# One run of small products a period: results of one pair of chunks together with the scores of the next, and sums that change PSUM halves

## The chip, the cores and the metric

The kernel runs on one core of a Trainium2 chip. The metric is device time in microseconds (us); the figure shown for a kernel is the median of its runs. Engines are named as in the profile: PE (TensorE, the matrix products), DVE (VectorE), ACT (ScalarE), POOL (GpSimd) and SP (SyncE, which here only issues DMAs).

## What is computed

A recurrent retention block feeds a feed-forward block. Four batches, eight heads, 768 positions, head size 64; 3072 tokens, model width 512, inner width 2048.

```python
for t in range(S):
    state = gamma[None, :, None, None] * state + np.einsum('bhd,bhe->bhde', k[:, :, t], v[:, :, t])
    y[:, :, t] = scale * np.einsum('bhd,bhde->bhe', q[:, :, t], state)
...
x = np.ascontiguousarray(attn_out.transpose(0, 2, 1, 3)).reshape(B * S, H * D)
...
h = x @ w_in
sp = np.maximum(h, 0.0) + np.log1p(np.exp(-np.abs(h)))
g = h * erf(sp)
return (g @ w_out).astype(np.float32)
```

## The kernel before, in words

**Chunks and groups.** The positions are cut into 24 chunks of 128 (six a batch). Two chunks make a group of 256 tokens, so there are 12 groups. A chunk j of the retention is done in two steps with small f32 products of 64x64 on PE.

- `begin(j)` (L560 to L576) makes the scores (L566, kT by qT) and the new contributions to the state (L573, k by v) for both halves of 64 positions. They fill two banks of PSUM.
- `states(j)` (L578 to L593), on DVE, masks the scores into `am` (L582) and adds the contributions to the running state (L591, L593).
- `results(j)` (L595 to L631) multiplies q with the state (L611) and the masked scores with v (L622) into two banks, and ACT copies the result to `xT` (L630). The second half's share of the first half's keys lies in a part of the bank of its own; `crossed_sums` (L633) adds it on DVE (L639, L641).
- `split_x` (L643) splits `xT` into three parts, x_hi on ACT (L314), x_lo and x_dif on DVE (L315, L316), in a ring of three groups.

**Units and periods.** From group 2 on, the hidden layer is computed in units. A unit (`pair_unit`, L712) multiplies two groups of tokens, 512 columns, with 128 columns of w_in in 12 products of 128x512 (L720): eight into one bank (the hi and lo parts) and four into a second (the dif part). Its `put` (L728) reads both banks, the first on ACT (L322), the second on DVE (L323), into a buffer `h` in SBUF, and POOL issues its store (L731). Period g is eight units (`period`, L936; periods 2 and 12 have four units of `unit`, L687, each with 24 products of 256 columns, L693). The periods' loop stands from L1000 on. What goes with each unit is written by hand in `period`: one table of PE work ahead of a unit, one of work for the other engines behind it. Every engine executes its own queue in that order.

In the periods 3 to 9 the table `joined` puts `begin` of both chunks ahead of unit 2, and their `results` ahead of unit 5, so PE leaves the large products twice in a period. In period 10 the two chunks go one by one, four runs of small products. The chunks up to 9 are done alike in both kernels.

**PSUM.** There are eight banks. The units' sums use the four of `ps_o` (o0 to o3), two at a time in turn (`banks`, L680); the retention's scores and results use two banks called hp and two called r.

**Preparation.** `load_pair` (L145) loads k and v of two chunks as they are through POOL's queue (L143, L153), and k and q once more in blocks of 32 through SP's queue (L159, 32 small DMAs a pair), in the units 0 to 2 of the period before their use. `prepare` (L531) transposes the blocks on DVE (L543), scales q (L538), and scales v on ACT (L550, sixteen small instructions a pair). Between all this, DVE and ACT turn w_out from 64-bit into 32-bit numbers in steps (`convert`; DVE lines L230, L244, L249, L253, L265, one step each, five a piece of weights); POOL loads its raw quarters (L208) and stores the pieces (L271).

**Buffers.** `h`, the masks `am` and the output rows share six small buffers of SBUF; most other tiles share 34 larger ones.

**The end.** After the units come the products with w_out (L905), 48 blocks of 24 products, fed by softplus and erf on ACT (L846, L850), a product on DVE (L860) and the same three-way split.

Of the kernel before, what the change touches and what calls it, by code (L numbers as in the profile page):

```python
# [21 lines left out]
P = 128  # L22
C = 128
# [26 lines left out]
def kernel(  # L50
# [39 lines left out]
    def b4(name, shape, dtype=F32):  # L90
        return big.tile([P] + shape, dtype, name=name, tag="b4")
# [22 lines left out]
    def of_chunk(x, j):  # L114

        b, c = divmod(j, NC)
        return x[b, :, c * C : (c + 1) * C, :].rearrange("h p d -> p h d")
# [24 lines left out]
        V[j] = VP[j - j % 2][:, j % 2]  # L142
        queue.dma_start(V[j], of_chunk(v, j))  # L143

    def load_pair(j):  # L145

        b, c = divmod(j, NC)
        KNP[j] = b4("kn", [2, H, D])
        KB[j], QB[j] = (b4(name, [HP, 2 * C]) for name in ("kb", "qb"))
        for i in range(2):  # L150
            load_values(j + i, nc.gpsimd)
            KN[j + i], SLOT[j + i] = KNP[j][:, i], head
            nc.gpsimd.dma_start(KN[j + i], of_chunk(k, j + i))  # L153
        yield
        for to, src in ((KB[j], k), (QB[j], q)):
            for s, d in itertools.product(range(2), range(2)):
                part = slice((2 * s + d) * 32, (2 * s + d + 1) * 32)
                for u in range(HP):
                    nc.sync.dma_start(  # L159
                        to[part, u].rearrange("p (a d) -> p a d", d=32),  # L160
                        src[b, head(u, s), c * C : (c + 2) * C, d * 32 : (d + 1) * 32].rearrange(
                            "(a p) d -> p a d", p=32
                        ),
                    )
                yield

    kq_s = const.tile([P, NC, 2, H], F32, name="kq_s")
    d_k = const.tile([P, H], F32, name="d_k")
# [362 lines left out]
    def prepare(j):  # L531


        for name, store, x in (("k", KT, KB[j]), ("q", QT, QB[j])):
            if name == "q":
                own = x.rearrange("p u (a d) -> p u a d", d=32)
                scale = kq_b[:, 1, :, j % NC : j % NC + 2].rearrange("p u c a -> p u (c a)")
                nc.vector.tensor_tensor(  # L538
                    own, own, scale[:, :, :, None].to_broadcast([P, HP, 8, 32]), op=ALU.mult
                )  # L540
                yield
            t = b4(name + "T", [HP, 2 * C])
# [3 lines left out]
            yield  # L546
        for i in range(2):
# [9 lines left out]
    def additions(j):  # L557
        return range(2 if j % NC < NC - 1 else 1)

    def begin(j, pool=ps_h, names=None):  # L560

        SC[j] = [ret_psum(pool) if names is None else ps_o.tile([P, HP, C], F32, name=names[r]) for r in range(2)]
        for hp in range(HP):
            for a, s in itertools.product(range(2), range(2)):
                t, own = slice(a * D, (a + 1) * D), slice(s * D, (s + 1) * D)
                nc.tensor.matmul(  # L566
                    SC[j][s][t, hp, :D], KT[j][own, hp, t], QT[j][own, hp, t], start=True, stop=True,
                )
        for u in range(HP):
            for r in range(2):  # L570
                for a in additions(j):
                    t = slice(a * D, (a + 1) * D)
                    nc.tensor.matmul(  # L573
                        SC[j][a][r * D : (r + 1) * D, u, D:], KN[j][t, SLOT[j](u, r), :], V[j][t, head(u, r), :],
                        start=True, stop=True,
                    )  # L576

    def states(j):  # L578

        AM[j] = b2("am", [2, HP, D])  # L580
        for s in range(2):
            nc.vector.tensor_tensor(  # L582
                AM[j][:, s],
                SC[j][s][:, :, :D],
                causal_d[:, None, :].to_broadcast([P, HP, D]),
                op=ALU.mult,
            )
        for a in additions(j):
# [6 lines left out]
    def results(j, names=None, pool=ps_r):  # L595

        x = x_of(j)
        pp = [ret_psum(pool) if names is None else ps_o.tile([P, HP, C], F32, name=names[r]) for r in range(2)]
        clear = set()

        def first(*bank):
# [72 lines left out]
        for g in range(2):  # L674
            nc.gpsimd.dma_start(HID[g][:, ft], h[:, g])

    turn = itertools.cycle(range(2))
    last_turn = itertools.cycle((ps_r, ps_h, ps_o, ps_o))
# [113 lines left out]
    def steps(s, n=1):  # L792
# [1 line left out]
            next(s, None)  # L794

    pair = load_pair(JPC + 2)
    prep = prepare(JPC + 2)
    a, b = JPC, JPC + 1
    during = {
        1: [(load_block_scales,)],  # L800
# [10 lines left out]
        12: [(split_weights, 2), (steps, prep, 1)],  # L811
        13: [(steps, prep, 1)],
# [123 lines left out]
    def period(g, prep, next_prep):  # L936

        a, b = 2 * g + 2, 2 * g + 3
        one, two = partial(partial, unit), partial(partial, pair_unit)
        if g == G2:  # L940
            units = [one(g, n) for n in range(NPC // 2)]
            return units, {0: [(results, a), (results, b, None, ps_h)]}, {
                0: [(crossed_sums, a), (crossed_sums, b)],
                1: [(split_x, a, 2)],
                2: [(split_weights, 4)],
                3: [(steps, next_prep, 4)],
            }, range(4)
        if g < NG:
            units = [two(g - 1, ft) for ft in range(8 * (g % 2), 8 * (g % 2) + 8)]
        if g == G2 + 1:  # L950
            return units, joined(2, 5, g), {
                0: [(steps, prep)],
                1: [(split_weights, 5)],
                2: [(states, a), (states, b)],
                3: [(split_weights, 6)],
                4: [(split_weights, 7)],
                5: [(crossed_sums, a), (crossed_sums, b)],
                6: [(split_x, a, 2)],
                7: [(steps, next_prep, 1)],
            }, range(4)  # L960
        if g < NG - 2:
            return units, joined(2, 5, g), {
                0: [(steps, prep, 4)],
                1: [(convert, 2)],
                2: [(states, a), (convert, 1)],
                3: [(states, b), (convert, 1)],
                4: [(convert, 2 if g < 8 else 1)],
                5: [(crossed_sums, a), (crossed_sums, b)],
                6: [(split_x, a, 2)],
                7: [(steps, next_prep, 1 if g < NG - 3 else 4), (convert, 1)],  # L970
            }, LOADS.get(g, ())
        if g == NG - 2:
            return units, {1: [(begin, a)], 2: [(results, a)], 3: [(begin, b)], 5: [(results, b)]}, {
                0: [(steps, prep, 4), (load_w_out, 0)],
                1: [(states, a), (load_w_out, 1)],
                2: [(crossed_sums, a), (split_w_out, 0)],
                3: [(states, b), (split_x, a)],
                4: [(split_w_out, 1), (load_hiddens, 0)],
                5: [(crossed_sums, b)],
                6: [(split_x, b), (softplus, 0), (load_w_out, 2)],  # L980
                7: [(erf, 0), (gated, 0)],
            }, ()
        if g == NG - 1:
# [14 lines left out]
        }, ()  # L998

    for g in range(G2, NG + 1):  # L1000
        pair = load_pair(2 * g + 4) if 2 * g + 4 < NJ else iter(())
        next_prep = prepare(2 * g + 4) if 2 * g + 4 < NJ else iter(())
        units, pe, other, loads = period(g, prep, next_prep)
        for i, work in enumerate(units):
            for f, *args in pe.get(i, ()):
                f(*args)
            put = work()
            steps(pair, 3)
            for part in itertools.islice(quarters, loads.count(i)):
                load_quarter(part)  # L1010
            if g == NG - 1 and i % 2:
# [5 lines left out]
            put()  # L1017
            while behind:
                behind.pop(0)()
        prep = next_prep  # L1020
    split_w_out(7)

    for n in range(NG * NU):
# [63 lines left out]
```

## Time and profile before

| | us |
|---|---|
| median of 3 runs | 612.63 (612.61 to 612.93) |
| the profiled execution, its own time | 613.15 |
| its span in the profile | 611.4 |
| PE busy | 604.6 |
| DVE busy | 459.8 |
| ACT busy | 390.3 |
| POOL busy | 132.5 |
| median landing of a store of h (L731) | 4.1 |
| median landing of a block of k (L159) | 2.8 |

The profile is of one execution. The span runs from its first to its last instruction; what lies around it makes up the rest of the execution's own time. A busy time is the time in which an engine had an instruction in execution; matrix products overlap, so each shows a duration longer than its distance to the next one. The chain of waits follows the work that ended last back to the start. In a timeline row stand start and duration in us, engine, line, operation, output and input tiles, shape and count; a bracket at its end tells how long the engine had been idle and what ended that.

### The profile page before, as it was taken

What the parts mean: (1) busy time and instruction counts of PE and PEld (TensorE: products, weight loads), DVE (VectorE), ACT (ScalarE), POOL (GpSimd) and SP (SyncE); (2) the same over time, 40 slices, a digit from 0 to 9 for tenths busy, and PEclk for the clock granted to TensorE, in tenths of its full rate; (3) what the DMA queues carried; (4) which work ended last, traced back from release to release, by engine and by line L of the source; (5) the groups of instructions that cost most, each with busy time, mean ns of one, the idle gap of its engine ahead of it and who ended that gap; (6) DMA issues with size and microseconds to landing.
All of it is one profiled execution on the core that took longest, in us unless ns stands there. A gap on an engine that the chain in (4) does not pass through costs nothing.

```text
span 611.4 us, 13214 instructions
## 1 busy us (share of the span) xinstructions
PE 604.6 (99%) x5222; PEld 507.3 (83%) x5222; DVE 459.8 (75%) x581; ACT 390.3 (64%) x614; POOL 132.5 (22%) x228
## 2 busy tenths in 40 slices
PE   8999999999999999999999999999999999999997
PEld 7888889888888888888788988888888888888886
DVE  5899988886978679787768978686776768668640
ACT  3667446354453634345387699889789888988920
POOL 1087435443526535241112200000000000000000
PEclk9999999999999999999999999999999999999999
DMA  9999659977979998894645834325324333531300
GB/s 203 312 263 281 149 132 248 265 161 221 219 201 277 269 270 182 243 233 151 215 143 187 286 119 148 127 70 173 103 88 154 106 129 110 172 119 55 103 35 34
DMA packets 143949, 106.28 MB, mean 174 GB/s; under 512 B 103056, under 2 KB 123792, under 8 KB 143888
## 3 DMA queue, kind: packets, MB, share of 16 engines
q1 hardware_dynamic: 128160, 58.09, 37.4%
q0 software_dynamic: 15168, 47.21, 24.6%
q8 instruction: 41, 0.67, 0.5%
q10 hardware_dynamic: 560, 0.14, 0.1%
q14 instruction: 20, 0.16, 0.1%
HBM read 69.75 MB, written 35.65 MB: 172 GB/s over the span
## 4 chain that ended last, share of the span: by engine, by line
PE 96%; SPq 2%; DMA 1%; ACT 0%; DVE 0%; issue 0%; DVEq 0%
PE o L720 31%; PE o L905 21%; PE r L905 11%; PE hp L905 11%; PE hp L665 9%; PE o L693 3%; PE hp L566 1%; DMA raw<-in_moe_w_in_dram 1%; PE hp L720 1%; PE r L720 1%; PE r L566 1%; PE r L611 1%; SPq L136 1%; PE r L622 1%; PE r L573 1%; PE hp L611 1%
## 5 line engine op out<-in xcount | busy, mean ns | idle before, releaser
L720 PE MATMUL o<-x_hi,w_hi 128*128 128x512 f32 x272 | 108.0, 397 | 0.0
L322 ACT ACTIVATE h<-o 128x512 f32<-128x512 f32 x74 | 43.8, 595 | 98.7 <-PE o L720 89.3
L720 PE MATMUL o<-x_lo,w_lo 128*128 128x512 f32 x272 | 106.0, 390 | 0.0
L860 DVE TENSOR_TENSOR e<-hid,e 128x1024 f32<-128x1024 f32 x48 | 56.7, 1222 | 61.9 <-ACT e L850 61.9
L323 DVE SCALAR_TENSOR_TENSOR h<-o,h 128x512 f32<-128x512 f32 x74 | 50.5, 686 | 34.3 <-ACT h L322 24.8
L720 PE MATMUL o<-x_dif,w_dif 128*128 128x512 f32 x272 | 72.7, 389 | 0.0
L731 POOL DMA_DIRECT2D hids<-h x72 | 39.6, 550 | 131.2 <-DVE h L323 123.1
L316 DVE SCALAR_TENSOR_TENSOR g_dif<-g_hi,g_lo 128x1024 fp32r<-128x1024 f32 x48 | 58.8, 1226 | 3.3
L720 PEld LDWEIGHTS o<-x_hi,w_hi 128*128 128x128 f32 x272 | 51.0, 188 | 11.4
L720 PEld LDWEIGHTS o<-x_dif,w_dif 128*128 128x128 f32 x272 | 51.1, 188 | 10.6
L314 ACT ACTIVATE g_hi<-e 128x1024 fp32r<-128x1024 f32 x48 | 51.0, 1062 | 13.5 <-DVE e L860 11.6
L720 PEld LDWEIGHTS o<-x_lo,w_lo 128*128 128x128 f32 x272 | 51.1, 188 | 10.1
L315 DVE TENSOR_TENSOR g_lo<-e,g_hi 128x1024 fp32r<-128x1024 f32 x48 | 58.6, 1221 | 0.5
L665 PE MATMUL hp<-xT,w 128*128 128x256 f32 x256 | 57.2, 381 | 0.0
L665 PEld LDWEIGHTS hp<-xT,w 128*128 128x128 f32 x256 | 48.0, 190 | 6.6
L846 ACT ACTIVATE e<-hid 128x1024 f32<-128x1024 f32 x48 | 48.2, 1052 | 0.3
L850 ACT ACTIVATE e<-e 128x1024 f32<-128x1024 f32 x48 | 48.2, 1052 | 0.3
L905 PE MATMUL o<-w_hi,g_hi 128*128 128x512 f32 x120 | 46.7, 389 | 0.0
L905 PE MATMUL o<-w_lo,g_lo 128*128 128x512 f32 x120 | 46.7, 389 | 0.0
L905 PE MATMUL o<-w_dif,g_dif 128*128 128x512 f32 x120 | 46.7, 389 | 0.0
L550 ACT ACTIVATE v<-v,kq_s 128x64 f32<-128x64 f32 x144 | 35.6, 335 | 0.0
L846 ACT ACT_TABLE_LOAD x24 | 30.8, 1283 | 0.5
(201 smaller groups left out, 1265.6 us busy)
## 6 DMA issues: line engine op xcount, KB each, us to landing
hids<-h POOLq DMA_DIRECT2D x72, 256.0 KB, 4.1
hid<-hids SPq DMA_DIRECT2D x36, 512.0 KB, 4.6
raw<-in_moe_w_in_dram SPq DMA_DIRECT2D x32, 256.0 KB, 5.5
raw<-in_moe_w_out_dram POOLq DMA_DIRECT2D x32, 256.0 KB, 6.2
hid<-hid SPq DMA_DIRECT2D x12, 512.0 KB, 5.2
out_dram<-y SPq DMA_DIRECT2D x23, 256.0 KB, 2.1
kb<-in_k_dram SPq DMA_DIRECT2D x144, 32.0 KB, 2.8
v<-in_v_dram POOLq DMA_DIRECT2D x18, 256.0 KB, 6.0
```

Of the source, the lines that this page charges most:

```text
L314: nc.scalar.activation(hi, x, AF.Copy, scale=KEEP)
L315: nc.vector.tensor_tensor(lo, x, hi.bitcast(F32), op=ALU.subtract)
L316: nc.vector.scalar_tensor_tensor(dif, hi.bitcast(F32), Z, lo.bitcast(F32), op0=ALU.mult, op1=ALU.subtract)
L322: nc.scalar.activation(to, a, AF.Copy, scale=1 + 1 / Z)
L323: nc.vector.scalar_tensor_tensor(to, b, -1 / Z, to, op0=ALU.mult, op1=ALU.add)
L665: nc.tensor.matmul(HP_[ft][:, g], w[:, kk, ft % 2 * P : (ft % 2 + 1) * P], XC[g][:, kk], start=(kk == 0), stop=(kk == n_k - 1),)
L720: nc.tensor.matmul(to, W[n][i][:, kk * 2 * P + u * P : kk * 2 * P + (u + 1) * P], XR[i][:, at, kk], start=(kk == 0 and i == parts[0]), sto ...
L731: nc.gpsimd.dma_start(HID2[g][:, ft % 8], h)
L846: nc.scalar.activation(E[n], HID_[n], AF.Softplus)
L850: nc.scalar.activation(E[n], E[n], AF.Erf)
L860: nc.vector.tensor_tensor(E[n], HID_.pop(n), E[n], op=ALU.mult)
L905: nc.tensor.matmul(Y[g][t][x // 2], G[n][x][:, f, t * P : (t + 1) * P], W_OUT[ft // 2][x][:, ft % 2 * d_model : (ft % 2 + 1) * d_model], s ...
```

## The change

The chunks of a pair and of the next pair meet in one run of small products. Ahead of unit 7 of the periods 4 to 9, a new function makes the `results` of the pair a, b and right behind them `begin` of the pair a + 2, b + 2. The results of chunk a + 2 are so multiplied a whole period after its scores. Periods 3 and 4 still begin their chunks ahead of unit 2; period 10 only makes the results of the last pair, ahead of unit 1.

The banks are no longer tied to a use. They form two halves (o0 to o3; hp and r). The units' sums use one half in turn. At each run the results go into the other half, the next scores go into the half that the sums used so far, and the sums move to the half of the results.

`states` is cut into `masks` and `add_states`, `prepare` into blocks (`prepare`) and values (`prepare_values`). The masks and states of the first chunk of the next pair stand behind unit 7, on either side of the split of x; those of its second behind unit 0 of the next period. The split moves from behind unit 6 to behind unit 7. The blocks of k and q are loaded from unit 5 on for a pair two periods on, k and v as they are after the blocks of k. The scaling of v is cut in two halves, behind units 3 and 4. Conversion steps and raw quarters of w_out are dealt anew: fewer in periods 4 and 5, eight steps in each of 6 to 9.

```diff
+    def results_and_begin(j):
+
+        old, i = home[0], turn[0]
+        home[0], turn[0] = 1 - old, 0
+        for c in range(2):
+            results(j + c, pp=two_banks(1 - old, c, [P, HP, C]))
+        for c in range(2):
+            begin(j + 2 + c, pp=two_banks(old, (i + c) % 2, [P, HP, C]))
+        for c in range(2):
+            crossed_sums(j + c)
...
+    def two_banks(half, i, shape):
+        if half:
+            return [(ps_h, ps_r)[i].tile(shape, F32, name=("hp", "r")[i]) for _ in range(2)]
+        return [ps_o.tile(shape, F32, name=f"o{2 * i + b}") for b in range(2)]
...
-        pool = next(last_turn) if last else ps_o
-        own = next(turn) if pool is ps_o else None
-        names = [f"o{2 * own + i}" if pool is ps_o else "hp" if pool is ps_h else "r" for i in range(2)]
-        return [pool.tile([P, 2, GT], F32, name=name) for name in names]
+        if last:
+            return two_banks(*next(last_turn), [P, 2, GT])
+        i = turn[0]
+        turn[0] = 1 - i
+        return two_banks(home[0], i, [P, 2, GT])
...
-    LOADS = {4: (3, 4, 5, 6), 5: range(2, 8), 6: (0, 1, 4, 5, 6, 7), 7: (2, 3, 4, 5), 8: (1, 2, 3, 4)}
+    LOADS = {5: (2, 2, 3, 3), 6: (2, 2, 3, 3, 4, 4, 5, 5), 7: (3, 3, 4, 4), 8: (0, 0, 1, 1, 4, 4, 5, 5)}
...
         if g < NG - 2:
-            return units, joined(2, 5, g), {
-                0: [(steps, prep, 4)],
-                1: [(convert, 2)],
-                2: [(states, a), (convert, 1)],
-                3: [(states, b), (convert, 1)],
-                4: [(convert, 2 if g < 8 else 1)],
-                5: [(crossed_sums, a), (crossed_sums, b)],
-                6: [(split_x, a, 2)],
-                7: [(steps, next_prep, 1 if g < NG - 3 else 4), (convert, 1)],
+            n = 1 + int(g > G2 + 3)
+            return units, {7: [(results_and_begin, a)]}, {
+                0: [(states, b)],
+                1: [(convert, n)],
+                2: [(convert, n)],
+                3: [(convert, n), (steps, next_values, 1)],
+                4: [(steps, next_prep, 1), (convert, 1), (steps, next_values, 1)],
+                5: [(steps, next_prep, 2)],
+                6: [(convert, 1)],
+                7: [(masks, a + 2), (split_x, a, 2), (add_states, a + 2)],
             }, LOADS.get(g, ())
         if g == NG - 2:
-            return units, {1: [(begin, a)], 2: [(results, a)], 3: [(begin, b)], 5: [(results, b)]}, {
+            return units, {1: [(results, a, None, ps_h), (results, b, None, ps_r)]}, {
...
+            if i == 5 and G2 + 2 <= g < NG - 3:
+                pair = load_pair(2 * g + 6, False)
             put = work()
-            steps(pair, 3)
+            steps(pair, 2 if i in (5, 6) else 3)
```

More of the change, by code (lines that the diff above doesn't have):

```diff
@@ L165, in load_pair @@
                 yield
+            if src is k and not first:
+                natural()
     kq_s = const.tile([P, NC, 2, H], F32, name="kq_s")
@@ L578, in states, with masks @@
     def states(j):
+        masks(j)
+        add_states(j)
+    def masks(j):
         AM[j] = b2("am", [2, HP, D])
@@ L593, in states, with results @@
                 nc.vector.tensor_tensor(to, x, new, op=ALU.add)
-    def results(j, names=None, pool=ps_r):
+    def results(j, names=None, pool=ps_r, pp=None):
         x = x_of(j)
-        pp = [ret_psum(pool) if names is None else ps_o.tile([P, HP, C], F32, name=names[r]) for r in range(2)]
+        pp = pp or [
+            ret_psum(pool) if names is None else ps_o.tile([P, HP, C], F32, name=names[r]) for r in range(2)
+        ]
         clear = set()
@@ L951, in period @@
             return units, joined(2, 5, g), {
-                0: [(steps, prep)],
+                0: [(steps, values)],
                 1: [(split_weights, 5)],
@@ L1000 @@
     for g in range(G2, NG + 1):
-        pair = load_pair(2 * g + 4) if 2 * g + 4 < NJ else iter(())
-        next_prep = prepare(2 * g + 4) if 2 * g + 4 < NJ else iter(())
-        units, pe, other, loads = period(g, prep, next_prep)
+        if g <= G2 + 2:
+            pair = load_pair(2 * g + 4, g < G2 + 2)
+        next_prep, next_values = (f(2 * g + 4) if 2 * g + 4 < NJ else iter(()) for f in (prepare, prepare_values))
+        units, pe, other, loads = period(g, prep, next_prep, values, next_values)
         for i, work in enumerate(units):
```

67 lines of the change are left out of this document (42 added, 25 removed).

## The prediction

> **What bounds the kernel now.** I read the page's first two parts, then the chain that ended last, the waits, and the timeline of PE.
>
> ```profile
> span 611.4 us, 13214 instructions
> PE 604.6 (99%) x5222; PEld 507.3 (83%) x5222; DVE 459.8 (75%) x581; ACT 390.3 (64%) x614; POOL 132.5 (22%) x228
> PE   8999999999999999999999999999999999999997
> PEclk9999999999999999999999999999999999999999
> PE 96%; SPq 2%; DMA 1%; ACT 0%; DVE 0%; issue 0%; DVEq 0%
> ```
>
> PE is busy in every slice at full clock and is 96% of the chain. A busy PE is not PE at its peak, so the waits come next. Asked for PE alone they name four groups, 2.9 us in all, and the timeline puts the last of them at 18.95 us. From there to the end nothing makes PE wait: **the time is the sum of what PE executes**, and a change pays only by what it takes out of that stream or by the waits that it puts in. The timeline of PE shows what a run of small products costs. Columns: start, duration, engine, line, operation, tiles, count of records (an f32 product of 64x64 has two).
>
> ```profile
> 211.93 1.07 PE L720 MATMUL o<-x_dif,w_dif 128*128 128x512 f32 x4
> 212.93 0.69 PE L566 MATMUL hp<-qT,kT 64*64 64x64 f32 x32
> 213.44 0.65 PE L573 MATMUL hp<-v,kn 64*64 64x64 f32 x32
> 213.91 0.65 PE L566 MATMUL r<-qT,kT 64*64 64x64 f32 x32
> 214.38 0.64 PE L573 MATMUL r<-v,kn 64*64 64x64 f32 x16
> 214.94 0.50 PE L720 MATMUL o<-x_hi,w_hi 128*128 128x512 f32 x1
> 215.28 0.39 PE L720 MATMUL o<-x_lo,w_lo 128*128 128x512 f32 x1
> ...
> 288.83 0.69 PE L566 MATMUL hp<-qT,kT 64*64 64x64 f32 x32
> 289.34 0.65 PE L573 MATMUL hp<-v,kn 64*64 64x64 f32 x32
> 289.92 0.50 PE L720 MATMUL o<-x_hi,w_hi 128*128 128x512 f32 x1
> ```
>
> Starts, not durations, count here. Inside the run a group of 32 records starts 0.47 us after the one before it; the first takes 0.51 and the last 0.56, and the first large product after it takes 0.34 instead of 0.23.
>
> **The price of a run's two edges.** Between runs stand stretches of units: 13.83 us for five units (199.10 to 212.93) and 8.39 for three (214.94 to 223.33). The difference of two units is 5.44, so a unit is 2.72, three are 8.16, and 0.23 us of each stretch is edge. The run for two chunks takes 2.01 us (212.93 to 214.94; 2.05 for the results at 223.33 to 225.38), the run for one chunk 1.09 (288.83 to 289.92). A chunk's share is so 0.92 to 0.96, mean 0.94, and 1.09 - 0.94 = 0.15 is edge inside the run. **One run costs 0.23 + 0.15 = 0.38 us beside its products.** Check: a period in steady state is 26.28 us (197.05 to 223.33); eight units 21.76 + four shares 3.76 + two edges 0.76 = 26.28.
>
> **What the change takes away.** The number of products stays (3251 rows on PE in both built programs); their order changes. In the order before I count 18 runs from period 3 on: two in each of periods 3 to 9, four in period 10. In the order after there are 10: two each in periods 3 and 4, one each in 5 to 9, one in 10. Eight runs fewer at 0.38 us: **-3.04 us**.
>
> The joint run has a seam that no row of before shows: results (L622) straight into scores (L566). The nearest row is the seam from L573 to L566 inside a run, 64x64 on both sides, with the usual 0.47: nothing. The other bound is a full edge, 0.38 on six joint runs, 2.3 us. I take nothing, since shape and type stay. [...]
>
> **What it adds and moves, and what hides it.** Let s be the start of a joint run. From the rows it lasts 2.05 + 2 x 0.94 = 3.93; unit 7 follows until s + 6.79 (a unit after a run takes 2.86, 199.10 to 201.96), then comes the next period's unit 0.
>
> *The split of x moves to the last moment.* Before, the results came before unit 5 and the split after unit 6. Now unit 0 reads x one unit after the run. The rows give the chain:
>
> ```profile
> 225.48 0.65 ACT L630 COPY xT<-r 128x256 f32<-128x256 f32 x2 [0.29 <-PE r L622]
> ...
> 226.16 0.48 DVE L641 TENSOR_TENSOR xT<-xT,r 128x128 f32<-128x128 f32 x2 [0.45 <-ACT xT L630]
> ...
> 228.02 1.06 ACT L314 ACTIVATE x_hi<-xT 128x1024 fp32r<-128x1024 f32 x1
> ...
> 229.11 1.23 DVE L315 TENSOR_TENSOR x_lo<-xT,x_hi 128x1024 fp32r<-128x1024 f32 x1
> 230.37 1.23 DVE L316 SCALAR_TENSOR_TENSOR x_dif<-x_hi,x_lo 128x1024 fp32r<-128x1024 f32 x1
> ```
>
> That run began at 223.33, so xT is ready at s + 3.31. x_hi takes until s + 4.4, x_lo until 5.7, x_dif until 6.95. The two masks of the next chunk now stand before the split on DVE: their products end about s + 2.9, two take 0.75 (L582), so they are over at 4.06, while ACT makes x_hi. Unit 0 needs x_lo in its second product, s + 7.0, and x_dif in its ninth, s + 8.6. **Slack 1.3 and 1.65 us: no wait.**
>
> *The halves of PSUM.* The results need the half that held the scores; masks and states read it a period ago. The scores need unit 5's and unit 6's sums read: the second pair starts at s + 2.9, and DVE finishes a sum about 0.94 after its unit (202.21 + 0.69 against 201.96), slack 1.9. Unit 7 writes where the first results stood: their last add ends at s + 2.4 (225.70), it starts at s + 3.93. Unit 1 needs unit 7's sum read: DVE does the split until 6.95, two state additions (0.86, L593) until 7.8, the sum until 8.45; unit 1 starts at 9.5, slack 1.05. After it two masks and two states (1.6) precede unit 0's sum, done at 10.7 for unit 2 at 12.2.
>
> *Behind the waits.* If a copy or mask waits longer, DVE's queue holds the sums behind it and POOL the stores of h behind those. DVE has room: 20.3 to 22.1 us busy in periods of 26.3 (the windows), plus at most two conversion steps of 0.69 to 1.22, about 23 of 25.9. I added up its queue with the pairs of steps (2.44) that periods 6 to 9 now put behind units 1 to 3, and with the transposes (2.45) behind unit 5: sums end at most 1.1 us later than now, and a bank is wanted 1.85 us after the present end.
>
> *Buffers of h.* Two masks now hold two of six for a whole period. h needs its own from the ACT read to the landing: 1.65 + 4.1, at worst 8.7 us, so 10.4; four units are 10.9.
>
> *Loads.* The blocks of k and q are issued a period ahead; the last, in unit 0, are wanted in unit 5, some 11.8 us on, against medians of 4 to 6 by period (one maximum of 14.5, the next 9.9). SP's order is unchanged; POOL issues k and v (0.9 each, 3.6 for four) between the stores of units 6 and 7, 5 us apart on DVE. The scaling of v on ACT splits from 3.9 us in one unit into two of 2. In period 4 v comes only about when ACT wants it: up to 1 us on ACT against 2 us until a bank is short. The w_out quarters come in pairs; one piece (period 6, units 2 and 3) is wanted by DVE some 9 us after its issue, with landings of 3.2 to 8.8. All of it nothing on PE.
>
> *The tail.* PE arrives 3 us earlier. The fifth block of g is split by 359.6 and used at 368.1, so 8.5 us ahead; the tail keeps its length.
>
> **Sum.** The profiled execution took 613.15 us around its span of 611.4: 613.15 - 3.04 = 610.1. The median of the runs shown, 612.63, lies 0.52 lower: **609.6 us**.
>
> **Rivals.**
> 1. *A recurring gap at the bank.* Sums and scores now share each half, so one late read in a period stops PE where it stopped nowhere. Smallest slacks: 1.05 us (unit 1) and 1.3 (x_lo). For it: every read hangs on one queue, DVE. Against: before most sums DVE still waited for ACT or PE, so it is seldom late. With 0.2 to 0.3 us in each of six periods 1.2 to 1.8 come back: 610.8 to 611.4. [...] Chance 0.12.
> 2. *The seam costs an edge, or the gap eats most.* The seam alone: -3.04 + 2.28, so 611.9. Against it: the 0.47 at L573 to L566. With larger gaps of rival 1 (0.4 to 0.7 a period) 612 to 613.8. Chance 0.09.
> 3. *Slower: DVE arrives at the run a conversion pair late.* Then the adds, the split and unit 0 slip together. It decides from 1.3 us of lateness; with a whole pair, 2.44, unit 0 waits 1.14 in six periods, 6.8 us: 616.4. More than 2.0 us late on each makes it slower than now. For it: periods 6 to 9 get one or two steps more, and one step stands behind unit 6. Against: my sum has DVE at most 1.1 late, and it waits 1 us in each run for the copies (225.22). Chance 0.09.
> That the change doesn't do what it says is excluded by the order on PE: the runs are there.
>
> **Numbers.** Forecast 609.6, own range 609.0 to 610.4, chance 0.70 (the edges of single runs scatter by 0.04, eight by 0.3). With rival 1 the range 609.0 to 611.4 holds 0.82. A measurement here tells about 0.2% (1.2 us) from no change: faster is forecast and rival 1, 0.82; same rival 2, 0.09; slower rival 3, 0.09.
>
> **What would show it.** Right: periods 5 to 9 last 25.9 us; groups inside the joint run start every 0.47, the seam included; PE has no waits there. Wrong: a gap before a unit's first product (banks, rival 1), a seam start of 0.6 or more (rival 2), x_lo ending after unit 0's start (rival 3), or PE waiting in scores for kT, qT or v.

## The result and the profile after

Over six executions the changed kernel took 620.80 us (618.64 to 621.89); the kernel before, beside it, 612.78 (612.61 to 613.05). The ratio is 1.0126, interval 1.0105 to 1.0147: **slower by 1.3%**, where 609.6 us was forecast. The profiled execution took 621.7 us. Line numbers from here on are those of the changed kernel: a pair unit is L763 (L720 before), scores L578, contributions to the state L585 (both begin), states' products L633 and masks' products L644 (both results).

The page of the changed kernel, the same parts as before:

```profile
span 620.0 us, 13215 instructions
PE 605.6 (98%) x5222; PEld 510.0 (82%) x5222; DVE 460.0 (74%) x579; ACT 390.7 (63%) x613; POOL 133.2 (21%) x228
PE   8999999999989999989999999999999999999997
PEclk9999999999999999989999999999999999999999
q8 instruction: 41, 0.67, 0.5%
PE 97%; issue 1%; DMA 0%; DVE 0%; ACT 0%; DVEq 0%
```

PE does what it did (605.6 us busy against 604.6), but the span is 8.6 us longer. Two slices of PE and one of its clock are no longer full, and the chain has 1% "issue": time in which PE waited for nothing that the profile shows. The waits of PE in the changed kernel (us in all, how often, longest; the row of L424 is of the kernel's start, as is one of 0.3 us that is left out):

```profile
PE o L578 <- issue: 3.1, 1, 3.1
PE r L585 <- issue: 2.1, 1, 2.1
PE o L424 <- POOL ident masks.py:199: 1.5, 1, 1.5
PE hp L585 <- issue: 1.4, 1, 1.4
PE o L585 <- issue: 1.3, 1, 1.3
PE o L763 <- issue: 0.8, 1, 0.8
```

Five stops are new, and none has a semaphore as releaser: no bank, no x_lo, no kT. Four stand inside a joint run (periods 4, 5, 7, 8), the fifth in the unit right behind that of period 9 (its second boundary lies 19 instructions behind the run). The longest, in the timeline of PE in period 8:

```profile
260.24 0.65 PE L644 MATMUL r<-am,v 64*64 64x64 f32 x32
260.71 0.65 PE L578 MATMUL o<-qT,kT 64*64 64x64 f32 x32
261.17 0.65 PE L585 MATMUL o<-v,kn 64*64 64x64 f32 x32
261.64 0.63 PE L578 MATMUL o<-qT,kT 64*64 64x64 f32 x29
265.34 0.33 PE L578 MATMUL o<-qT,kT 64*64 64x64 f32 x3 [3.07 <-issue]
265.46 0.69 PE L585 MATMUL o<-v,kn 64*64 64x64 f32 x32
266.09 0.50 PE L763 MATMUL hp<-x_hi,w_hi 128*128 128x512 f32 x1
```

The seam (L644 to L578, 260.24 to 260.71) is the 0.47 that was forecast. PE then stops after the 29th record of a group, in the middle of one chunk's scores, whose first 29 records had all they needed. What arrives then is instructions. The DMA view of 262.0 to 264.5 us in the changed kernel has one transfer on that queue (packets, MB, share of the time):

```profile
q8 instruction: 1, 0.02, 2.8%
```

Its record runs from 262.81 to 263.92; PE goes on at 265.34. On the page the queue has 41 transfers, 0.67 MB: 16 KB each. PE has 5222 products and 5222 weight loads, 10444 instructions, and 10444 / 41 is 255; with the 71 semaphore and drain records of its queue it is 256.5. **A transfer holds 256 instructions of PE.** Counted in the trace with these records, each of the five stops comes after the same number of records modulo 256, 193 (after 3777, 4545, 5825, 6593 and 7361: 3, 5, 3 and 3 times 256 apart), and each ends 1.3 to 1.5 us behind the landing of such a transfer.

**Where the 8.55 us came from** (621.70 - 613.15, profiled executions). From start to start the five stops are 1.51, 2.30, 1.61, 3.29 and 1.22: 9.93, less 0.3 of ordinary spacing. Behind the longest the granted clock was 0.50 for 3.41 us (266.98 to 270.39):

```profile
266.00:270.40 4.40, 4.40 (x23) 3.45 (x16) 0.52 (x2) 0.60 (x1) 0.00 (x0) 0.61 0.74 135
270.40:280.00 9.60, 9.60 (x44) 7.92 (x43) 8.38 (x13) 2.84 (x4) 2.20 (x4) 1.00 0.49 135
```

(Windows view; the third number from the right is the granted clock.) The eight units there took 23.63 us instead of 21.98: 1.65 more. A block boundary in the second unit behind the run of period 6 cost 0.26 more, in pauses too short for the list of waits (the eight units there take 22.25 us). Together 9.63 + 1.65 + 0.26 = 11.54, so 11.54 - 8.55 = 2.99 us were won elsewhere. Of these 0.29 lie ahead of the first unit (90.58 us against 90.87), where nothing was changed. The eight runs fewer are left with 2.7, against 3.04 forecast.

### The profile page after: what moved, and what is told of

Read it like the earlier page. It is cut to its first block, busy times and chain, and to the rows that moved or that the text cites. A ratio compares the mean times of both kernels' runs of the same rounds, so it can differ in the third digit from the quotient of the medians.

```text
span 620.0 us, 13215 instructions
## 1 busy us (share of the span) xinstructions
PE 605.6 (98%) x5222; PEld 510.0 (82%) x5222; DVE 460.0 (74%) x579; ACT 390.7 (63%) x613; POOL 133.2 (21%) x228
## 4 chain that ended last, share of the span: by engine, by line
PE 97%; issue 1%; DMA 0%; DVE 0%; ACT 0%; DVEq 0%
PE o L948 21%; PE o L763 20%; PE hp L948 11%; PE r L948 11%; PE hp L687 9%; PE hp L763 7%; PE r L763 6%; PE o L736 3%; PE o L633 1%; PE r L472 1%; PE r L578 1%; PE o L511 1%; PE r L585 1%; PE o L644 1%; PE o L585 1%
## 5 line engine op out<-in xcount | busy, mean ns | idle before, releaser
L763 PE MATMUL o<-x_hi,w_hi 128*128 128x512 f32 x176 | 69.4, 394 | 0.0
L763 PE MATMUL o<-x_lo,w_lo 128*128 128x512 f32 x176 | 68.6, 390 | 0.0
L329 ACT ACTIVATE h<-o 128x512 f32<-128x512 f32 x50 | 29.6, 594 | 61.3 <-PE o L763 55.3
L330 DVE SCALAR_TENSOR_TENSOR h<-o,h 128x512 f32<-128x512 f32 x50 | 34.1, 685 | 24.4 <-ACT h L329 13.7
L763 PE MATMUL o<-x_dif,w_dif 128*128 128x512 f32 x176 | 47.2, 389 | 0.8 <-issue 0.8
L763 PEld LDWEIGHTS o<-x_dif,w_dif 128*128 128x128 f32 x176 | 33.0, 188 | 7.9 <-issue 1.0
L763 PEld LDWEIGHTS o<-x_hi,w_hi 128*128 128x128 f32 x176 | 33.0, 188 | 7.2
L763 PEld LDWEIGHTS o<-x_lo,w_lo 128*128 128x128 f32 x176 | 33.1, 188 | 6.6
```

The costliest lines, as they stand in the source:

```text
L330: nc.vector.scalar_tensor_tensor(to, b, -1 / Z, to, op0=ALU.mult, op1=ALU.add)
L763: nc.tensor.matmul(to, W[n][i][:, kk * 2 * P + u * P : kk * 2 * P + (u + 1) * P], XR[i][:, at, kk], start=(kk == 0 and i == parts[0]), sto ...
```

## The experiments

Theory: PE empties its instructions faster than blocks of 256 arrive. In units it takes 24 instructions in 2.72 us; in a run of small products 32 records of products (64 instructions) in 0.47 us, 137 a microsecond, and a block in 1.87 us. A run of 258 can use up only one block; a run of 483 to 516 meets a second boundary 256 instructions behind the first, and stops. The expectations assume that a block is asked for 320 instructions ahead of its boundary and arrives 4 to 6 us later (3.7 in the tail). No run shows when a block is asked for, so these are estimates: 320 instructions at 137 a microsecond are 2.33 us, which with the changed kernel's stops inside the joint runs, 1.5 to 3.3 us, makes 3.8 to 5.6. The traces show the transfer (0.96 to 1.77 us at the five stops) and the 1.3 to 1.5 us from its landing to PE's next record. Main rivals: the banks and the change of halves; the order of the loads; the traffic alone. Each ratio is to the kernel before, measured beside the run (medians 612.8 to 613.1).

**1. Cut the run** (results stay ahead of unit 7, begin goes ahead of unit 1 of the next period).

```diff
-            return units, {7: [(results_and_begin, a)]}, {
+            return units, {1: [(begin_alone, a)], 7: [(results_alone, a)]}, {
...
```

> The joint run is taken apart again: the results stand alone ahead of unit 7, the next scores ahead of unit 1 of the next period, two units later; halves of PSUM, loads, preparation and the late split of x stay as in the changed kernel. Sixteen runs of small products instead of 10 (before: 18). Fetch theory (PE runs out of instructions in a run of 512, because a block of 256 comes 4 to 6 us after it is asked for, and the run uses one up in 1.9 us): a run of 258 with two units behind it leaves over 7 us, so no stall; 612.8 - 2 x 0.38 = 612.0 us (611.6 to 612.6). Rival, the banks or DVE's queue (the sums wait for the shared halves, the late split stops unit 0): these waits stay, 617 us or more.

Measured: 619.11 us (618.47 to 620.26), ratio 1.0104 [1.009, 1.0118]. The time missed; the profile has no "issue" any more, but waits on semaphores, which the changed kernel didn't have:

```profile
PE o L770 <- ACT xT L652: 1.2, 2, 0.8
PE hp L770 <- DVE xT L663: 0.8, 2, 0.6
```

Unit 7 now follows the results at once and writes their banks, which the scores had covered. No test of the theory yet.

**2 to 4. Same instructions, other places of the boundaries.** PE no-ops behind units 0 to 6, and nothing else:

```diff
+  for _ in range(fill * (i + 1) // 7 - fill * i // 7 if i < 7 else 0):
+      nc.tensor.nop(hint="pad")
```

> The changed kernel with 483 empty instructions (no-ops) on PE, 72 to 93 in each of the periods 4 to 9, spread over the units 0 to 6. They do nothing but move the joint runs against the blocks of 256 instructions: a block now begins 20 instructions (34 in periods 4 and 7) into each joint run, so that the next one is asked for in the unit before. Fetch theory: 5.3 us or more between asking and need, against 4 to 6: no stalls or a few tenths in periods 4 and 7; 609.7 us (609.4 to 611), the time that the prediction gave. Rivals (data not ready, banks, DVE late, the seam): no-ops help none of them, 618 to 622 us as in the changed kernel.

> The changed kernel with 395 no-ops on PE, none in period 4, 58 to 93 in each of 5 to 9, placed so that a block begins 108 instructions into every joint run. Fetch theory: in each of the six runs 320 instructions, 2.33 us, between asking and need, so PE stops in all six of them, always 364 instructions after the start of the run, for the latency less 2.33 us: 1.6 to 3.6 us each, 9 to 20 in all; 609.7 + 9 to 20 = 619 to 630 us, likeliest 623. In the changed kernel only four of six stop. Rivals that do not know of instructions: as the changed kernel, 618 to 622, with stops in any place.

> Control: the kernel before, with the same 483 no-ops in the same places. It tells what a no-op costs by itself. If PE's sequencer takes them while the array works off its queue: 612.8 us as before (612.5 to 613.1). If each holds up the array by 15 ns or more: 620 us or more. Runs of 258 instructions leave about 8.9 us between asking and need wherever a block begins, so by the fetch theory moving them gives no stall either.

Measured: e2 613.75 (612.02 to 615.17), ratio 1.0013 [1.0004, 1.0023], 7 us less than the changed kernel; e3 627.46, ratio 1.0243 [1.0224, 1.0262]; e4 613.08, ratio 1.0001 [0.9991, 1.001]. The waits of PE in e3, then in e2:

```profile
PE o L585 <- issue: 4.3, 2, 3.3
PE o L578 <- issue: 3.4, 1, 3.4
PE hp L585 <- issue: 2.8, 2, 1.4
PE r L578 <- issue: 1.6, 1, 1.6
```

```profile
PE o L578 <- issue: 1.7, 1, 1.7
PE hp L687 <- ACT h L695: 1.2, 1, 1.2
PE r L644 <- issue: 0.7, 1, 0.7
```

In e3, inside its range, all six joint runs stop, each after 366 records, where the second boundary was put at 108 + 256 = 364. In e2 most are gone, though each of its runs still holds two boundaries, 20 or 34 instructions behind its start and 256 further on: it counts how early in the run they lie. Only no-ops tell these kernels apart, and in the kernel before as many cost nothing: the place of the block boundary sets the stop. e2 missed its number, since two stops and some small bank waits are left. The stop of 1.7 us is in period 6's joint run; that of 0.7 us is in the results' run of period 10, which has 258 instructions at most.

**5. Cut the run again, banks pinned** (hp and r for results and begin, o for the sums).

```diff
-            begin(j + 2 + c, pp=two_banks(old, (i + c) % 2, [P, HP, C]))
+        results(j, pool=ps_h)
+        results(j + 1)
...
+    def begin_alone(j):
+
+        begin(j)
+        begin(j + 1, ps_r)
...
```

> All of the change but one thing: the joint run is cut into two runs, results ahead of unit 7 and begin ahead of unit 1 of the next period, both in the four banks hp and r, while the sums of the units keep o0 to o3 and change nothing (so the bank waits of e1_two_runs can't come up). The order of the loads, the split of states into masks and sums, the values' steps and the place of the splits stay those of the changed kernel; the last period has begin ahead of unit 1 and results ahead of unit 3. Theory (PE runs out of instructions inside a run of 483 to 516 instructions, at the second boundary of a block of 256): no run has more than 258 instructions, so no stop with 'issue' as releaser; six more edges of 0.38 us than the 609.74 forecast: 612.0 us, between 611.6 and 612.8. Rival (the loss sits in the other parts of the change, the order of the loads or the work on DVE and ACT): 618 to 621 us, and waits of PE on semaphores.

Measured: 618.61 us (618.40 to 619.09), ratio 1.009 [1.0077, 1.0103]: missed. No "issue", but

```profile
PE o L764 <- DVE x_lo L322: 3.1, 6, 0.6
PE hp L949 <- DVE h L330: 1.5, 1, 1.5
```

The split of x has lost its cover. The prediction gave it 1.3 us of slack behind a joint run whose second half takes 1.88; without that half, 1.30 - 1.88 = -0.58, and PE waited 0.5 to 0.6 six times.

**6. The same, results one unit earlier** (results ahead of unit 6, x split behind it), so that the split has two units (the edit against run 5).

```diff
-            return units, {1: [(begin_alone, a)], 7: [(results_alone, a)]}, {
+            return units, {1: [(begin_alone, a)], 6: [(results_alone, a)]}, {
...
```

> e5_run_cut with results ahead of unit 6 instead of 7 and the split of x behind unit 6, so that two units lie between the results and the unit that takes the split x (in e5 one unit lay between and PE waited about 0.6 us for x_lo in each of six periods); in the last period begin stands ahead of unit 0 and results ahead of unit 2. All other parts of the change stay, the joint run alone is undone. Theory (only the length of the joint run does the harm): no stops, none of these waits, 12 more edges and 0.38 us each than the forecast allow 611.8 to 613.2 us, the time of the kernel before. If the other parts of the change cost something: above 614, with waits of PE that name it.

Measured: median 612.23 us, before 613.00 (nine of ten executions 611.94 to 613.14, one 618.26; ratio 0.9998 [0.9981, 1.0015]). The whole list of PE's waits:

```profile
PE o L424 <- POOL ident masks.py:199: 1.5, 1, 1.5
PE r L472 <- ACT kqT L466: 0.6, 2, 0.3
PE hp L460 <- DVE kq L445: 0.4, 2, 0.2
```

All are of the first 19 us. The order of the loads, the cut of states in masks and sums, the values' steps: in this execution they cost 0.6 us, in one stretch of period 8 (253.53 to 262.52), where weight loads waited for x_lo and for h, too short for this list. The execution of 618.26 has no profile; that the order of the loads costs something now and then isn't ruled out. This kernel has 16 runs against 18 before; two edges are 0.76 us and the medians differ by 0.77, with an interval of 1 us on either side. Of the 8 us that the changed kernel lost, only the joining, with the change of halves that goes with it, is left as the cause; experiment 8 has neither.

**7. What the traffic does.** First, transfers moved away from the units ahead of the run, with and without no-ops:

```diff
-  LOADS = {5: (2, 2, 3, 3), 6: (2, 2, 3, 3, 4, 4, 5, 5), 7: (3, 3, 4, 4), 8: (0, 0, 1, 1, 4, 4, 5, 5)}
+  LOADS = {5: (2, 2, 3, 3), 6: (2, 2, 3, 3, 7, 7, 7, 7), 7: (3, 3, 3, 3), 8: (0, 0, 1, 1, 7, 7, 7, 7)}
...
-  if i == 5 and G2 + 2 <= g < NG - 3:
+  if i == 7 and G2 + 2 <= g < NG - 3:
...
-  steps(pair, 2 if i in (5, 6) else 3)
+  steps(pair, 3)
```

> The kernel of e2_aligned (block boundary 20 or 34 instructions into each joint run) with transfers taken out of the two units ahead of the run: the loads of the next chunks' q and k start behind the run instead of two units ahead of it, the quarters of w_out that stood behind units 4 and 5 stand behind unit 7, and the values' steps come a unit later. Theory with contention (e2's two stops are late blocks: the transfer of 16 KB waited behind the other transfers, DMA engines 90 to 99% busy): the stops of 1.7 and 0.7 us go, 609.7 to 611.5 us. If the DMA traffic has no part in it: the stops stay, 613 to 614 us. If DVE or ACT get late by the moved loads: semaphore waits of PE instead, 611 to 614.

> The changed kernel without the no-ops, with only the moves of transfers of e6_aligned_moved. Boundaries lie where they lay in the changed kernel (364, 425, 352 and 410 instructions into the runs of the periods 4, 5, 7 and 8). Theory: the stops stay at the same instructions, since 320 instructions take only 2.3 us inside the run and a block takes 3.7 us even when the DMA engines are quiet (the tail of the changed kernel), but each is about 1.4 us long instead of 1.6 to 3.1, none is long enough for the half clock: 615 to 618 us. If the traffic has no part: 620 to 622. If the stops come from the traffic alone: 610 to 611.

Measured: 639.36 and 639.94 us, ratios 1.0412 [1.0376, 1.0447] and 1.044 [1.0424, 1.0455], both far outside. DVE waited for q (in e6):

```profile
DVE qb L545 <- DMA qb<-in_q_dram: 25.8, 4, 8.6
```

and PE for qT behind it, up to 5.2 us, then in part at half clock (mean granted clock of the run 0.983). The two units' head start of the loads is needed; nothing follows on the blocks. Then fewer packets for q and k (1 KB in a row instead of 128 bytes), then also the quarters moved, with and without no-ops, and the quarters alone (the moves of LOADS as above; e8, e9 and e10 read q and k from other places and so leave out the right placement, e12 doesn't):

```diff
-  to[part, u].rearrange("p (a d) -> p a d", d=32),
-  src[b, head(u, s), c * C : (c + 2) * C, d * 32 : (d + 1) * 32].rearrange(
-      "(a p) d -> p a d", p=32
+  to[part, u].rearrange("p (a d) -> p a d", d=64),
+  src[b, head(u, s), c * C + d * C : c * C + (d + 1) * C, :].rearrange(
+      "(p a) d -> p a d", p=32
```

> The kernel of e2_aligned with the loads of q and k blocks (kb, qb) reading 1 KB in a row per partition instead of eight pieces of 128 bytes: the same bytes into the same tiles, an eighth of the packets, from other places (the placement of q and k that the reference needs is left out). Nothing else moves. Theory with contention: the DMA engines are less busy ahead of the runs, the two late blocks of e2 come in time, 609.7 to 611.5 us. If the traffic has no part: 613 to 614.

> e8_aligned_light (no-ops that put a block boundary 20 or 34 instructions into each joint run; q and k blocks read in rows of 1 KB, their placement left out) with one thing more: the quarters of w_out that were issued behind units 4 and 5 of the periods 6 and 8 are issued behind unit 7, so that the two units ahead of the runs of these periods hold 1 MB less traffic. In e8_aligned_light the DMA engines were still 95 to 102% busy there and the stops of 1.7, 1.4 and 0.7 us stayed. Theory with contention (the block of instructions waits its turn among the other transfers): the stops in the runs of the periods 6 and 8 go, 609.7 to 611.5 us, below the kernel before. If the traffic has no part in it: stops at the same places, 613 to 614 us.

> e9_aligned_quiet without the no-ops: the changed kernel with light q and k loads (placement left out) and the quarters moved; the boundaries lie where they lay in the changed kernel. Theory: with less traffic a block still takes some 3.7 us from being asked for, and inside the run 2.3 us lie between asking and need, so the stops stay in the periods 4, 5, 7 and 8 at the same instructions, each 1 to 2 us, and none of 3 us: 614 to 618 us. If the stops were the traffic's doing alone: 610 to 611. If the traffic has no part: 620 to 622.

> e2_aligned, with q and k loaded as the reference needs them, and only the quarters of w_out of the periods 6 and 8 moved from behind the units 4 and 5 to behind unit 7. The loads of q and k stay where the change put them, so that e6's wait for q can't come from their delay. Theory with contention: e2's stop of 1.7 us in period 6 goes or shrinks, 610 to 612.5 us, a version that beats the kernel before or equals it; but 1 MB more is in flight while q and k load, and if q then comes late to the DVE as in e6, PE waits for qT and it is 614 to 625. If the traffic has no part: 613.75 as e2.

Measured: e8 613.34, ratio 1.0002 [0.9991, 1.0013], missed, in its rival's range; e9 612.58 (610.92 to 614.82), 0.9994 [0.9983, 1.0005], above its range; e10 617.08 (616.12 to 619.12), 1.0078 [1.0063, 1.0093], inside; e12 614.77, 1.0023 [1.0011, 1.0034], with one stop of 0.4 us left and a wait of 1.4 for qT in place of the others. The windows of 199 to 205 us, ahead of and in period 6's run, in e2, e8 and e9 (DMA share is the last number but one):

```profile
199.00:205.00 6.00, 5.74 (x154) 4.74 (x153) 4.66 (x7) 3.21 (x7) 2.36 (x5) 1.00 1.08 347
```

```profile
199.00:205.00 6.00, 4.69 (x149) 3.86 (x148) 3.56 (x8) 3.15 (x7) 2.22 (x4) 1.00 1.00 374
```

```profile
199.00:205.00 6.00, 6.00 (x250) 5.34 (x248) 3.87 (x10) 3.37 (x7) 2.87 (x4) 1.00 0.80 238
```

With 1.08 and 1.00 that run stopped for 1.7 us, with 0.80 not at all. e8's fewer packets had left the engines as full as they were, so it is no test. In e9 two stops of 0.5 us were left in the joint runs of the periods 7 and 9, and one of 1.8 us in the run of period 10, two units behind the last joint run. That run stopped in e2, e6, e7, e8 and e10 too, for 0.3 to 2.6 us. The sharper pair is the changed kernel and e10, with the boundaries at the same instructions:

```profile
PE hp L585 <- issue: 1.5, 1, 1.5
PE o L578 <- issue: 1.0, 1, 1.0
PE o L585 <- issue: 1.0, 1, 1.0
PE r L585 <- issue: 1.0, 1, 1.0
```

The same four runs stop after the same 366, 427, 354 and 412 records, for 1.0 to 1.5 us instead of 1.3 to 3.1. Three are shorter; that of period 7 is not (1.5 for 1.4), and there the DMA share during the stop hardly changed (0.74 for 0.78). Within the changed kernel the four stops grow with it: 1.3, 1.4, 2.1 and 3.1 us at 0.47, 0.78, 0.85 and 1.07. So traffic lengthens the stops; it doesn't make them.

**8. The kernel before, made to stop.** No-ops in a burst, then small products:

```diff
+  for _ in range(256 if i == 5 and G2 + 2 <= g < NG - 2 else 0):
+      nc.tensor.nop(hint="pad")
```

> The kernel before, with its own runs of 224 to 258 products' instructions, and 256 no-ops in one go right behind the results' run (ahead of unit 5) in each of the periods 4 to 9: 482 to 514 instructions in a row with no joint run, no change of halves and no other load. e4_before_noops, with 483 no-ops 11 at a time behind units, took the time of the kernel before. Theory (PE eats instructions faster than the blocks of 256 arrive, whatever the instructions are): the no-ops' own time, 256 x 7 ns = 1.9 us a period if they pass as fast as the small products do, 11 us, and stops of 1 to 3 us in most of the six periods that end some 1.4 us behind the landing of a block of instructions, shorter where a boundary lies early in the run (35 and 50 instructions, two of the six) than where it lies late: 620 to 640 us. Rival (the stops need the joint run's products, their banks or operands): the same gap, the no-ops' own time, in all six periods whatever the boundary, 613 to 625 us.

Measured: 737.95 us, ratio 1.2041 [1.2024, 1.2057], far outside. The gap is 18.7 us in all six periods, as here in period 5:

```profile
193.01 0.67 PE L622 MATMUL r<-am,v 64*64 64x64 f32 x32
212.14 0.76 PE L720 MATMUL o<-x_hi,w_hi 128*128 128x512 f32 x1 [18.46 <-issue]
```

18.46 / 256 is 72 ns for a no-op, ten times a small product's instruction. The six gaps are alike (111.2 us of waits in all, the longest 18.6), whatever the place of the boundary, and the run says nothing on the theory. So the products themselves:

```diff
+        for _ in range(1 + (10 <= j < 22)):
+            for hp in range(HP):
...
```

> The kernel before, with every product of begin issued twice in a row for the chunks 10 to 21 (six runs): the second pass writes the same values to the same places, so nothing waits for anything new. The six runs of begin have 450 or 514 instructions instead of 226 or 258, in their old places, banks and order of loads; no joint run, no change of halves, no no-ops. The products' own time: 4 x 1.88 + 2 x 1.65 = 10.8 us, 623.7 us. Theory (the second block boundary inside a long run of small products stops PE): boundaries at 321, 412, 338 and 429 instructions into the four runs of 514, and 4 and 21 instructions behind the two of 450: stops with 'issue' as releaser of 1 to 3 us in the four, perhaps a shorter one behind the 450s, all some 1.4 us behind the landing of 16 KB of instructions: 628 to 638 us. Rival (the stops belong to the joint run of the change, its operands, banks or the change of halves): no stops, 623 to 624.5 us.  e14_before_burst did not tell these apart: the no-ops took 72 ns each, slower than blocks arrive.

Measured: 662.94 us, ratio 1.0822 [1.0803, 1.0842]; the direction of the theory, and 25 us beyond its range. The waits of PE and one run of the timeline:

```profile
PE r L574 <- issue: 10.9, 2, 5.8
PE r L567 <- issue: 10.3, 2, 5.4
PE o L721 <- issue: 4.8, 2, 3.0
```

```profile
168.12 0.69 PE L567 MATMUL hp<-qT,kT 64*64 64x64 f32 x32
...
170.04 0.65 PE L567 MATMUL r<-qT,kT 64*64 64x64 f32 x32
176.46 1.12 PE L574 MATMUL r<-v,kn 64*64 64x64 f32 x30 [5.78 <-issue]
```

No joint run, no change of halves, the old loads: **all six runs stop**. The four of 514 instructions do after 322, 414, 340 and 430 records; 321, 412, 338 and 429 were computed. The two of 450 stop among the large products right behind the run, where the boundary was computed 4 and 21 instructions behind it. That settles it for the theory. The size was wrong because the four stops inside a run are 5.1 to 6.0 us from start to start, not 1 to 3, with half clock around them (mean granted clock of the run 0.975). They lie where the next loads of q and k are under way: the DMA share during them is 1.09 to 1.13, above that of the changed kernel's longest stop. Taken together, the kernels here with a joint or a doubled run have 38 stops of PE over 0.15 us with "issue" as releaser behind their first 25 us; the others without no-op bursts have none. All 38 come after 193 records modulo 256, and all end 1.2 to 1.6 us behind the landing of a block.

**9. Joint runs only where blocks come in time.**

```diff
+  pe = {7: [(results_and_begin, a)]} if g in JOINT else {6: [(results_alone, a)]}
```

> Joint runs only where e2_aligned had no stop and no traffic stood in the way: in the periods 4, 5 and 7, each with no-ops ahead of it that put a block boundary 34 or 20 instructions behind its start. In the periods 6, 8 and 9 the run is cut as in e11_run_cut_early (results ahead of unit 6, begin ahead of unit 1 of the next period, both in the half of the banks that the sums don't use). Theory (the harm is a block that comes late inside a long run, and a run of 258 is safe at any place): no stop with 'issue', three edges of 0.38 us fewer than e11_run_cut_early, whose median was 612.23 us: 611.1 us, between 610.6 and 612.0, faster than both kernels. If the length of a run is harmful of itself, or the change of halves is: at or above 613.

> e13_three_joint without the joint run of period 7, the one in which a stop (1.1 us) was left: joint runs in the periods 4 and 5 alone, with the no-ops ahead of them, and cut runs in 6 to 9. Theory: no stops; two edges of 0.38 us fewer than e11_run_cut_early (612.23): 611.5 us, between 611.0 and 612.6; if the blocks of these two runs come late in some executions, up to 613.

Measured: three joint runs 613.05 us (611.54 to 614.41), ratio 1.0002 [0.9993, 1.0011], missed, and at the lower end of its rival's: the joint run of period 7 still stopped for 1.1 us, and the run of begin ahead of unit 1 of that period for 0.2. Its profile doesn't speak for the rival: from the first unit to the products with w_out it takes 255.32 us, e11 255.27. Without its two stops (1.7 us from start to start) and e11's 0.6 us, the three joint runs are 1.0 us ahead, where 1.14 was forecast. Two joint runs (periods 4 and 5): **611.73 us, before 612.79, ratio 0.9979 [0.997, 0.9988]**, a version that beats both kernels, by 0.2% against the kernel before. Eleven of its twelve executions lie between 610.95 and 612.77. The profiled one took 619.17: there DVE waited 4.9 us for a load of period 8, where nothing is joined, and PE 2.4 and 1.2 for h behind it. A stop of 0.2 us was left in the joint run of period 4.

## Why the prediction was wrong

- *What failed.* "From there to the end nothing makes PE wait: the time is the sum of what PE executes", with the waits listed under "What it adds and moves" and closed with "All of it nothing on PE". Every wait weighed was one on a semaphore. PE's own instructions, a transfer like any other, had no term, and the change alters just what decides it: how many of them PE takes at 137 a microsecond without a pause. The missing term is 9.6 us of stops and 1.65 of half clock, against a gain of 3.04; experiments 2 to 4 and 8 show that it hangs on where the boundaries of 256 instructions lie.
- *It stood in the profile of before.* Its page has the instruction queue too (41 transfers, 0.67 MB), 5222 products and as many weight loads, and the 0.47 us a group was the prediction's own row. 516 instructions in one go are two blocks. How late a block comes then, no run of before could show: none of its runs holds two boundaries.
- *The edge of 0.38 us was near.* -3.04 forecast; the changed kernel's sum leaves -2.7, 0.34 a run. From the start of one joint run to that of the next it takes 25.8 to 26.0 us less its stops, where 25.9 was forecast. The medians of the cut run with two runs fewer (-0.77 for -0.76) and of the version with four fewer (-1.06 for -1.52) agree with that, but with intervals of 1 and 0.5 us on either side they don't measure it.
- *The seam held*: 0.46 to 0.47 in all six runs.
- *The slacks held.* No wait on banks, x_lo or h in the changed kernel; and where e5 took the cover away, the wait was the one that the slack gives.
- *Rivals.* None was this one. Rival 3, slower by a late DVE, had the sign but no trace of its mechanism; rival 1's recurring gap exists, but at no bank.
- *Open.* When a block is asked for is in no record. In the products with w_out of the changed kernel, from 370 us on, a transfer's record starts 287 to 299 records ahead of the boundary that it serves, 3.6 to 4.8 us before PE enters the block ahead; at the five stops it starts only 0 to 149 records ahead of the boundary. In e2 four of the six transfers for the second boundaries still start before PE reaches the first; the one behind the stop of 1.7 us starts 1.4 us after it. This fits that a boundary early in the run leaves part of the wait to the unit ahead, but no run tests it alone. Why the run of period 10 stops at all, behind two units of large products (1.8 us in e9, at a DMA share of 0.81), wasn't settled.

## What to carry to other kernels

Count the instructions of a stretch, not only its time: weight load and product each count, an f32 product of 64x64 four in all. Inside the joint runs PE took 256 of them in 1.87 us and stood for 1.2 to 3.3 us (start to start) at five of the six second boundaries, in or just behind the run; so a gain of 2.7 us became a loss of 8. Compare the instruction queue's transfers with PE's instruction count before merging runs of small products, and leave a stretch of large ones inside every 256 or so; two units (48 instructions, 5.4 us) were enough behind the cut runs of e11, and not behind the last joint run of e9. A wait with no releaser, in the middle of a group whose operands are old, is to be looked for on the instruction queue: count the records ahead of it modulo 256.

## What the hardware showed beyond that

- A block boundary cost nothing inside stretches of large products (the kernel before takes 41 blocks, and no wait of PE comes later than 18.95 us) and up to 6.0 us, start to start, inside or just behind long runs of small ones.
- The half clock lasted 3.41 us behind the stop of 3.07, 6.83 around that of 5.78 (mean granted clock of e15 0.975), 17.1 or 20.5 around the bursts of 18.46 (of e14 0.919): the longer ones are 2, 5 and 6 times 3.41. Behind the stop of 3.07 us the half clock cost 1.65 more. The length of a stop doesn't decide it alone: one of 1.77 us in e9 had 3.41 us of half clock behind it, one of 2.08 in the changed kernel none.
- A PE no-op takes 72 ns when nothing hides it, and 10 to 14 of them behind a unit of 2.72 us cost nothing (e4: 613.08 us).
